# The second dense layer of a fused attention and rational FFN kernel: all blocks in float16 parts, scales from bounds on GpSimd, a new order

## The chip, the cores and the metric

The kernel runs on one core of a Trainium2 chip. The metric is the device time of one execution in microseconds. The core has a matrix engine (PE, with its weight loads PEld), a vector engine (DVE), a scalar engine (ACT), GpSimd (POOL) and a queue engine (SP). Each works through its own instructions in order, and semaphores join them. PE multiplies from SBUF into the eight banks of PSUM.

## The reference

```
# q, k, v: batch 8, heads 8, sequence 576, head size 64
scores = q @ k^T / 8
scores = where(scores >= max(scores) - tau, scores, -1e9)       # tau = 0.02
attn = exp(scores - max); attn = attn / (sum(attn) + 1e-9)
x = (attn @ v), heads side by side: 4608 tokens x 512
h = x @ w_in                                                    # 512 x 2048
P = a0 + a1 h + a2 h^2 + a3 h^3;  Q = 1 + |b0| |h| + |b1| h^2
out = (P / (Q + 1e-6)) @ w_out                                  # 2048 x 512
```

All inputs are float32. The weights come as raw 64-bit words (float32 values widened), which the kernel decodes on the chip.

## The kernel before, in words

**Attention.** Two heads of a batch make a pair; a pair has four full tiles of 128 query rows and a short one of 64, so there are 160 units of (pair, tile). For each, PE forms the scores (lines 805, 812, 816), DVE takes the row maxima (822 for two heads, 824 for a short tile), ACT applies threshold and exponential (837, 841), and the result is split into a float16 high part (`hi`, helper lines 326 and 328) and a low part (863, in place in `e`). SP's queue transposes both with DMAs into `pT`, and PE multiplies with v's parts (934). The output is stored as two float16 parts `x` (944, 950); the short tiles of four batches share one buffer `xr`. The first four pairs take another way with float32 transposes on PE (886 to 917).

**Dense layers.** The tokens are worked in 18 chunks of 256: two per batch (`m`) and two of short rows (`r`, four batches each). A chunk has four steps of four blocks (128 hidden columns each). In a step PE makes h from `x` and `wi`, both in float16 parts, with three products per block and quarter (line 1051, 48 matmuls of 256 columns a step). ACT takes h out of PSUM into one of eight buffers `t` (1060). DVE and ACT work out P/Q: |h| (1065 or 1067), r and q (1071, 1074, 1084, 1087 to 1093), log and exp for the reciprocal (1078, 1081). The second layer sums into two banks: one block of four is multiplied as plain float32 (1114), the other three as fp32r parts (1110), for which `g` is split in pieces of 256 columns: a cast (318 on ACT, 320 on DVE) and a low part (1101).

**Weights.** Each of 32 tiles is loaded on GpSimd's queue and decoded on ACT and DVE. A tile of w_in gets its size (544 or 546), a scale per group of four over a small PE product (431 to 440), and two float16 parts (326 or 328, and 562). A tile of w_out stays float32, or is cast and subtracted into two fp32r parts (592).

**Order.** All work is given to a planner as operations with a key, a duration, the engines that may do it and the buffers that it takes. The planner lays them out by its own clock, and each engine's instructions stand in that order in the program. Its parameters are constants at the head of the file: `WHEN` is the key of each weight group, `SPACING` that between dense steps, `START`, `EARLY` and `PRICE` weigh ACT against DVE for work that either can do, and `LAST` lists the chunks whose steps get keys behind the attention. Before, these were all three chunks left in the last batch (two `m` and the second `r`).

Lines that the working uses, with their numbers:

```
1051  nc.tensor.matmul(d, wi_tile(c, f0 + j, hl), x[:, c, :], ...)          # 3 parts x 4 quarters
1101  nc.vector.tensor_tensor(fr(g[:, 1]), box["r"][:, j * CT:(j + 1) * CT], g[:, 0], ALU.subtract)
1110  nc.tensor.matmul(acc[tt], fr(g[:, x]), fr(wo[f][y]), ...)             # 3 products of fp32r parts
1114  nc.tensor.matmul(acc[tt], box["r"][:, o:o + P], wo[f], ...)           # float32
```

Of the kernel before, what the change touches and what calls it, by code (L numbers as in the profile page):

```python
# [9 lines left out]
F32R = mybir.dt.float32r  # L10
# [16 lines left out]
POOLS = {"e": 3, "hi": 2, "pT": 2, "st": 8, "sc": 2, "t": 8, "u": 3, "g": 2, "x": 3, "xr": 1}  # L27
# [4 lines left out]
LEAD, SPACE0, SPACING = 4.776489494, 2.7365, 2.085146464  # L32
ENDK, ENDS = 4.7452, 10.130284218

WHEN = [(-4.7413, 1.6268), (5.5534, 0.8332), (13.0267, 0.2709), (15.0744, 0.5122)]

V0, V1 = -3.870384768, -4.680004432
# [6 lines left out]
LAST = (0, 1, 2)  # L44
# [12 lines left out]
PARTS = 3  # L57
# [5 lines left out]
PLAIN = (0, 1, 2, 3, 4)  # L63
# [4 lines left out]
AHEAD_RANK = 2.6679  # L68
# [43 lines left out]
class Hold:  # L112
# [3 lines left out]
    def __init__(self, pool, uses, sets=None):  # L116
        self.pool, self.uses, self.until, self.sets, self.bank, self.slot = pool, uses, 0.0, sets, None, None


class Plan:  # L120
# [28 lines left out]
    def spot(self, h, t):  # L149

        if h.sets is None:
            slots = self.pools[h.pool]
            return min(slots) if slots else None
        got = [(max([t] + [self.banks[i] for i in b]), n, b) for n, b in enumerate(h.sets)
               if all(self.banks[i] is not None for i in b)]
        return min(got)[::2] if got else None

    def sooner(self, e, t, o, free, can):
        price = START if t < START_END else EARLY if t < EARLY_END else PRICE
        for x, dur in o.engs.items():  # L160
            if x != e:
                begin = max(free[x], o.ready[x])
# [5 lines left out]
    def order(self):  # L168
# [21 lines left out]
        while left:  # L190
# [60 lines left out]
            for h in o.drop:  # L251
# [5 lines left out]
                elif not h.uses:  # L257
                    self.pools[h.pool].append((h.until, h.slot))
# [18 lines left out]
def masked_attention_rational_ffn(  # L277
# [54 lines left out]
    def tensor_tensor(dst, x, y, how):  # L332
# [28 lines left out]
    ones = bass.AP(one.tensor, one.offset, [list(one.ap[0]), [0, P]])  # L361

# [26 lines left out]
    def monic():  # L389
# [6 lines left out]
        nc.vector.tensor_tensor(t, b1, t, ALU.max)  # L396
        nc.vector.reciprocal(u, t)
# [14 lines left out]
    def scale_ops(key, get, up, inv, s, after, ahead=0.0):  # L412
# [20 lines left out]
        def f3():  # L433
            p2 = box["p2"]
            nc.vector.tensor_reduce(box["m2"], box["all"], AX.X, ALU.max)
            nc.vector.tensor_single_scalar(p2.bitcast(I32), box["m2"].bitcast(I32), 0x7F800000, ALU.bitwise_and)
            nc.vector.tensor_scalar(p2, p2, 2.0 ** -40, 2.0 ** 100, ALU.max, ALU.min)
# [30 lines left out]
    def decode_ops(i, key, load, hold, dst=None):  # L468
# [49 lines left out]
        o6 = op(FLEX["f6"], 0, key, f6, [o4, o2], (), [ht] if dst is None else [ht, hold])  # L518
# [778 lines left out]
```

## Time and profile before

| | us |
|---|---|
| median of 3 runs (1277.5 to 1283.15) | 1280.21 |
| the profiled execution | 1281.68 |
| its span, first to last instruction | 1279.9 |
| PE busy, 9252 matmul records | 1246.4 |
| DVE busy, 1960 instructions | 1199.3 |
| ACT busy, 2180 instructions | 1074.5 |
| POOL busy | 231.3 |

The granted clock of PE is 0.994 over the span. In a row of a stretch stand its bounds and length, then each engine's busy time with its count of instructions, the granted clock, the share of the DMA engines and GB/s. A row of a group has line, engine, operation, tiles written and read, shapes and count, then busy time and mean length in ns, then the idle time ahead of it and what ended that. A row of the timeline or of the chain of waits begins with start and length in us.

### The profile page before, as it was taken

To read this page: it belongs to the slowest core of one execution; us is meant where nothing else is said; L and a number is where in the kernel's file an instruction comes from. 1 tells how busy PE (TensorE), PEld (TensorE's weight loads), DVE (VectorE), ACT (ScalarE), POOL (GpSimd) and SP (SyncE) were. 2 spreads that over 40 slices of the span, in tenths; PEclk is the share of its full clock that TensorE was granted. 3 is DMA by queue.
4 is the path that set the end of the run, shared out by engine and by line. 5 is a ranking of instruction groups with operands and counts; after the bars stand their busy time and mean duration, and the time that the engine had idled before them with its cause. 6 is when DMAs were issued, how large, how long until landed. Compare 5 with 4: busy or idle time off the path is not lost.

```text
span 1279.9 us, 25127 instructions
## 1 busy us (share of the span) xinstructions
PE 1246.4 (97%) x9252; PEld 889.8 (70%) x9252; DVE 1199.3 (94%) x1960; ACT 1074.5 (84%) x2180; POOL 231.3 (18%) x480
## 2 busy tenths in 40 slices
PE   8899999999999999999999999999999999999998
PEld 6576676676767667766667667677776667677775
DVE  5899999999999999999999899999999999997876
ACT  5999888989999888888897699999988998874454
POOL 2112000132132311332022140322121221100000
PEclk9999999999999999999999999999999999999999
DMA  7645246688667656776442765876566665530000
GB/s 216 174 143 163 78 105 112 134 144 154 105 133 132 146 107 119 142 137 126 91 105 56 131 141 111 142 135 136 104 120 125 130 123 112 111 71 17 18 17 17
DMA packets 338251, 146.64 MB, mean 115 GB/s; under 512 B 314416, under 2 KB 320720, under 8 KB 338128
## 3 DMA queue, kind: packets, MB, share of 16 engines
q1 hardware_dynamic: 316528, 87.67, 38.5%
q0 software_dynamic: 21280, 56.78, 16.4%
q8 instruction: 73, 1.20, 0.4%
q10 hardware_dynamic: 320, 0.59, 0.2%
q14 instruction: 50, 0.41, 0.1%
HBM read 60.30 MB, written 9.44 MB: 54 GB/s over the span
## 4 chain that ended last, share of the span: by engine, by line
PE 53%; DVE 27%; ACT 8%; issue 5%; DMA 3%; SPq 0%; DVEq 0%; ACTq 0%
PE banks L1051 16%; PE banks L1110 15%; PE banks L1114 6%; PE banks L934 6%; PE banks L816 5%; DVE e L863 4%; DVE st L822 3%; DMA pT<-e 2%; DVE t L1071 2%; DVE t L1087 2%; DVE t L1090 2%; PE banks L805 2%; DVE t L1084 2%; DVE t L1093 2%; DVE g L1101 2%
## 5 line engine op out<-in xcount | busy, mean ns | idle before, releaser
L1051 PEld LDWEIGHTS <-wi 128*128 128x128 f16 x3456 | 324.1, 98 | 144.1 <-issue 108.0
L1051 PE MATMUL banks<-x,wi 128*128 128x256 f16 x3072 | 374.7, 275 | 3.0 <-ACT t L1060 1.7
L1110 PE MATMUL banks<-wp,g 128*128 128x512 f32 x1296 | 355.2, 415 | 1.9 <-ACT g L318 1.2
L1110 PEld LDWEIGHTS banks<-wp,g 128*128 128x128 f32 x1296 | 234.0, 189 | 70.9 <-issue 15.5
L837 ACT ACTIVATE e<-banks,st 128x576 f32<-128x576 f32 x288 | 206.4, 735 | 18.5 <-DVE st L831 11.1
L841 ACT ACTIVATE e<-e,cf 128x576 f32<-128x576 f32 x288 | 221.0, 774 | 0.3
L863 DVE SCALAR_TENSOR_TENSOR e<-e,st,hi 128x576 f16<-128x576 f32 x252 | 203.5, 808 | 3.9 <-ACT hi L326 3.4
L822 DVE TENSOR_REDUCE st<-banks 128x2 f32<-128x1152 f32 x128 | 171.8, 1342 | 12.9 <-PE banks L816 10.8
L326 ACT ACTIVATE hi<-e,st 128x576 f16<-128x576 f32 x177 | 134.0, 769 | 51.9 <-DVE st L852 41.1
L816 PE MATMUL banks<-KK,QQ 64*128 64x512 f32 x512 | 144.5, 641 | 0.0
L1114 PE MATMUL banks<-wp,t 128*128 128x512 f32 x288 | 142.2, 608 | 1.7 <-DVE t L1093 1.6
L1060 ACT ACTIVATE t<-banks,hsc 128x512 f32<-128x512 f32 (+1 forms) x192 | 106.3, 575 | 25.9 <-PE banks L1051 24.7
L934 PEld LDWEIGHTS <-V 128*64 128x64 f16 x2520 | 104.1, 111 | 33.8 <-issue 32.6
L934 PE MATMUL banks<-pT,V 128*64 128x256 f16 (+1 forms) x2520 | 118.9, 249 | 3.0 <-DMA pT<-e 3.0
L1087 DVE SCALAR_TENSOR_TENSOR t<-t,co,t 128x1024 f32<-128x1024 f32 (+1 forms) x73 | 92.0, 1261 | 22.7 <-ACT t L1081 22.7
L1078 ACT ACTIVATE t<-t,co 128x1024 f32<-128x1024 f32 (+1 forms) x73 | 82.7, 1133 | 12.8 <-DVE t L1084 12.7
L1093 DVE SCALAR_TENSOR_TENSOR t<-t,co,t 128x1024 f32<-128x1024 f32 (+1 forms) x73 | 92.0, 1261 | 0.5
L1071 DVE SCALAR_TENSOR_TENSOR t<-t,co 128x1024 f32<-128x1024 f32 (+1 forms) x73 | 92.0, 1260 | 0.0
L1084 DVE SCALAR_TENSOR_TENSOR t<-t,co,t 128x1024 f32<-128x1024 f32 (+1 forms) x73 | 91.9, 1260 | 0.0
L1074 DVE SCALAR_TENSOR_TENSOR t<-t,co 128x1024 f32<-128x1024 f32 (+1 forms) x73 | 91.9, 1259 | 0.0
L1101 DVE TENSOR_TENSOR g<-t,g 128x256 fp32r<-128x256 f32 x216 | 86.6, 414 | 2.0 <-ACT g L318 1.6
L1090 DVE SCALAR_TENSOR_TENSOR t<-t,t 128x1024 f32<-128x1024 f32 (+1 forms) x73 | 87.7, 1201 | 0.4
(137 smaller groups left out, 1518.2 us busy)
## 6 DMA issues: line engine op xcount, KB each, us to landing
KK<-in_kT_dram POOLq DMA_DIRECT2D x84, 144.0 KB, 3.9
t<-in_w_in_dram POOLq DMA_DIRECT2D x16, 512.0 KB, 5.8
t<-in_w_out_dram POOLq DMA_DIRECT2D x16, 512.0 KB, 4.7
V<-in_v_dram POOLq DMA_DIRECT2D x24, 256.0 KB, 4.4
out_dram<-u POOLq DMA_DIRECT2D x24, 256.0 KB, 2.7
QQ<-in_qT_dram POOLq DMA_DIRECT2D x42, 144.0 KB, 3.1
QQ<-in_qT_dram POOLq DMA_DIRECT2D x42, 128.0 KB, 3.4
KK<-in_kT_dram SPq DMA_DIRECT2D x24, 144.0 KB, 3.5
```

The lines of the kernel that those rows point to most:

```text
L326: nc.scalar.activation(dst, src, AF.Identity, scale=factor)
L816: nc.tensor.matmul(d, QQ[r, t * P:(t + 1) * P], KK[r, REM:S], **one)
L822: nc.vector.tensor_reduce(box["st"][:, 0:2], box["both"], AX.X, ALU.max, negate=True)
L837: nc.scalar.activation(ev(hh), box["s"][hh], AF.Prelu, scale=SCALE, bias=box["st"][:, 2 + hh:3 + hh], alpha=STEEP)
L841: nc.scalar.activation(e, e, AF.Exp, scale=passes, accum_out=box["st"][:, 4 + hh:5 + hh])
L863: nc.vector.scalar_tensor_tensor(box["lo"][:, c], ev(hh), box["st"][:, 6 + hh:7 + hh], box["hi"][:, c], ALU.mult, ALU.subtract)
L934: nc.tensor.matmul(dst, V[:, c * P + head * D:c * P + (head + 1) * D], rhs, start=c == 0 and n == 0, stop=c == NT and n == 2)
L1051: nc.tensor.matmul(d, wi_tile(c, f0 + j, hl), x[:, c, :], start=c == 0 and n == 0, stop=c == NC - 1 and n == 2)
L1071: nc.vector.scalar_tensor_tensor(box["r"], box["h"], a2, box["h"], ALU.add, ALU.mult)
L1087: nc.vector.scalar_tensor_tensor(box["q"], box["q"], qc, box["i"], ALU.add, ALU.mult)
L1110: nc.tensor.matmul(acc[tt], fr(g[:, x]), fr(wo[f][y]), start=begins and j == n == 0, stop=ends and j == nb - 1 and n == 2)
L1114: nc.tensor.matmul(acc[tt], box["r"][:, o:o + P], wo[f], start=begins and j == 0, stop=ends and j == nb - 1)
```

## The change

**Second layer.** Every block is multiplied as three products of float16 parts (new line 1153). g is cast into float16 (329 or 331) and its low part taken (1144) for a whole step at once, 1024 columns instead of 256, into three buffers `g` of 1024 columns. w_out is treated like w_in: size, scale per group, two float16 parts (339 or 337, and 610).

**Scales from bounds.** float16 has a small range, so g is scaled. A bound on |g| is worked out for each chunk's batch from a bound on |x|, on the columns of w_in and on the polynomial. The columns' norms come from squares that ACT leaves in bfloat16, summed by PE (596) and reduced on DVE (599 to 602). Per group of weights come seven small DVE instructions (1264 to 1270, three times in all), and per table, of which there are twelve, four on GpSimd (1293 to 1296), six on DVE (1299 to 1304) and one on ACT (1307). The scale enters through the bias of the exponential (1123), a factor at 1133 instead of -2, and the output's factor. Sizes of tiles are sums of squares on ACT in 24 cases, and maxima on DVE in eight.

**Buffers and order.** `t` has 12 slots instead of eight, in pairs that could be taken as one. In the last batch the short tiles come with the first half of the visits. `LAST` has only the second `m` chunk, whose last step is cut in two as before; the two other chunks get keys among the others. `SPACING` goes from 2.085 to 2.235, and `WHEN`, `START` and `PRICE` are set anew.

The core of the diff:

```diff
-LEAD, SPACE0, SPACING = 4.776489494, 2.7365, 2.085146464
+LEAD, SPACE0, SPACING = 4.776489494, 2.7365, 2.235134465
-LAST = (0, 1, 2)
+STEPS = {'m': (4, 4, 4, 4), 'r': (4, 4, 4, 4), 'last': (4, 4, 4, 2, 2)}
+LAST = (1,)
+REST_FIRST = (7,)
...
-             "g": ([P, 2, CT], F32), "x": ([P, 2, NP, CT], F16), "xr": ([P, 2, NP, CT], F16)}
+             "g": ([P, 2, NC * CT], F16), "x": ([P, 2, NP, CT], F16), "xr": ([P, 2, NP, CT], F16)}
...
-        def f_inv():
-            nc.scalar.activation(box["i"], box["i"], AF.Exp, scale=-1.0)
+        def f_inv(x, j0, j1):
+            i = box["i"][:, j0 * CT:j1 * CT]
+            nc.scalar.activation(i, i, AF.Exp, scale=-1.0, bias=lnr(x))
...
-        def f_gl(j):
-            g = box["g", j]
-            nc.vector.tensor_tensor(fr(g[:, 1]), box["r"][:, j * CT:(j + 1) * CT], g[:, 0], ALU.subtract)
+        def f_gl(x, j0, j1):
+            w = (j1 - j0) * CT
+            nc.vector.tensor_tensor(box["g", x][:, 1, 0:w], box["r"][:, j0 * CT:j1 * CT], box["g", x][:, 0, 0:w], ALU.subtract)
...
-            if in_parts(f):
-                g = box["g", j][:, :, tt * P:(tt + 1) * P]
-                for n, (x, y) in enumerate(((0, 0), (1, 0), (0, 1))):
-                    nc.tensor.matmul(acc[tt], fr(g[:, x]), fr(wo[f][y]), start=begins and j == n == 0,
-                                     stop=ends and j == nb - 1 and n == 2)
-                return
-            o = j * CT + tt * P
-            nc.tensor.matmul(acc[tt], box["r"][:, o:o + P], wo[f], start=begins and j == 0, stop=ends and j == nb - 1)
+            x = f // NC
+            o = (f - max(x * NC, f0)) * CT + tt * P
+            for n, (y, z) in enumerate(((0, 0), (1, 0), (0, 1))):
+                nc.tensor.matmul(acc[tt], box["g", x][:, y, o:o + P], wo[:, x, f % NC, z], start=begins and j == n == 0,
+                                 stop=ends and j == nb - 1 and n == 2)
...
+            def f_bound():
+                x = isx[:, b:b + 1] if kind == "m" else R
+                e = engines[plan.eng]
+                e.tensor_scalar(H, x, wmax, 1.0, ALU.mult, ALU.mult)
+                e.tensor_scalar(s, H, c2, H, ALU.add, ALU.mult)
+                e.tensor_scalar(s, s, c1, H, ALU.add, ALU.mult)
+                e.tensor_scalar(s, s, c0, ct, ALU.add, ALU.mult)
+
+            def f_scales():
+                nc.vector.scalar_tensor_tensor(s, H, c1s, s, ALU.add, ALU.min)
+                nc.vector.tensor_single_scalar(s.bitcast(I32), s.bitcast(I32), EVEN, ALU.bitwise_and)
+                nc.vector.tensor_scalar(s, s, SMALL, None, ALU.max)
+                nc.vector.tensor_scalar(R.bitcast(I32), s.bitcast(I32), -0.5, float(197 << 23), ALU.mult, ALU.add)
+                nc.vector.tensor_scalar(m2r, m2, R, None, ALU.mult)
+                nc.vector.tensor_scalar(down, s, dn, None, ALU.mult)
+
+            def f_ln_r():
+                nc.scalar.activation(lnr, m2r, AF.Ln, scale=-0.5)
...
+            o = op(BOUND, 0, p, f_bound, o)
+            o = op("DVE", 0.8, p, f_scales, [o])
+            o = op("ACT", 0.25, p, f_ln_r, [o])
```

What the order makes of it is shown at three places. First PE, where the attention's last product (`pT`, `V`) gives way to the dense layers alone. Before, it goes on with fp32r products (`wp_0`, `wp_1` are w_out's parts):

```order
L934 LDWEIGHTS V_165
L934 MATMUL banks<-pT_84,V_165 64x64
L1110 MATMUL banks<-wp_0_159,g_97 128x512 x2
L1110 MATMUL banks<-wp_1_160,g_97 128x512
L1110 MATMUL banks<-wp_0_159,g_97 128x512 x2
L1110 MATMUL banks<-wp_1_160,g_97 128x512
L1051 LDWEIGHTS wi
L1051 MATMUL banks<-x_100,wi 128x256
```

And now, on the same engine, with `wo` as w_out's float16 parts:

```order
L969 LDWEIGHTS V_141
L969 MATMUL banks<-pT_76,V_141 64x256
L1153 LDWEIGHTS g_88
L1153 MATMUL banks<-wo,g_88 128x512
L1153 LDWEIGHTS g_88
L1153 MATMUL banks<-wo,g_88 128x512
```

Behind this point stand 456 first-layer matmuls, 222 fp32r and 24 float32 products before, and 354 first-layer and 288 float16 products now. Behind the last scores (a little earlier) they are 552, 234 and 26 before, and 468 and 312 now.

Second, DVE in the third batch, behind the scale of v. Before, from the table of h's scales (`hsc`) it goes straight back to the attention:

```order
L863 SCALAR_TENSOR_TENSOR e_80<-e_80,st_86,hi_83 128x576
L950 SCALAR_TENSOR_TENSOR x_99<-banks,x_99 128x256
L1221 TENSOR_SCALAR hsc<-sw,isx 128x4
L852 RECIPROCAL st_87<-st_87 128x2
L822 TENSOR_REDUCE st_88<-banks 128x2
```

Now the table of the bounds (`gs`) follows it:

```order
L898 SCALAR_TENSOR_TENSOR e_72<-e_72,st_78,hi_75 128x576
L1336 TENSOR_SCALAR hsc<-sw,isx 128x4
L1299 SCALAR_TENSOR_TENSOR gs_m_0_4_156<-gs_m_0_4_156,co 128x1
L1300 TENSOR_SCALAR gs_m_0_4_156<-gs_m_0_4_156 128x1
L1301 TENSOR_SCALAR gs_m_0_4_156<-gs_m_0_4_156 128x1
L1302 TENSOR_SCALAR gs_m_0_4_156<-gs_m_0_4_156 128x1
L1303 TENSOR_SCALAR gs_m_0_4_156<-gc_4_151,gs_m_0_4_156 128x4
L1304 TENSOR_SCALAR gs_m_0_4_156<-gs_m_0_4_156,gc_4_151 128x1
```

Six instructions are new in DVE's row there; the first waits for POOL, each other one for the one ahead of it.

Third, POOL's queue at the same place, which before held loads of k, q and v alone (`KK`, `QQ`, `V`):

```order
L688 DMA KK_116<-in_kT_dram 64x576
L1293 TENSOR_SCALAR gs_m_0_4_156<-isx,gc_4_151 128x1
L1294 TENSOR_SCALAR gs_m_0_4_156<-gs_m_0_4_156,co 128x1
L1295 TENSOR_SCALAR gs_m_0_4_156<-gs_m_0_4_156,co 128x1
L1296 TENSOR_SCALAR gs_m_0_4_156<-gs_m_0_4_156,co 128x1
L724 DMA V_141<-in_v_dram 128x4x128
```

The first of the four waits for DVE's scale of v (`isx`), and the load of v stands behind them.

More of the change, by code (lines that the diff above doesn't have):

```diff
@@ L242, in order @@
                     slots = self.pools[h.pool]
-                    h.slot = min(slots)[1]
-                    slots.remove(min(slots))
+                    h.slot = self.spot(h, t)[1]
+                    slots[:] = [x for x in slots if x[1] != h.slot and not (h.wide and x[1] == h.slot + 1)]
                 else:
@@ L257, in order @@
                 elif not h.uses:
-                    self.pools[h.pool].append((h.until, h.slot))
+                    self.pools[h.pool] += [(h.until, h.slot + i) for i in range(1 + h.wide)]
             for d in o.then:
@@ L410, in masked_attention_rational_ffn, with bounds, scale_ops @@
     co = op("DVE", 2.1, 6.0, monic, [co])
-    def scale_ops(key, get, up, inv, s, after, ahead=0.0):
+    def bounds():
+        nc.vector.tensor_single_scalar(co_[:, 9:12].bitcast(I32), co_[:, 0:3].bitcast(I32), 0x7FFFFFFF, ALU.bitwise_and)
+        nc.vector.tensor_scalar(c1s, ct, 1.0, 0.25, ALU.add, ALU.mult)
+        nc.vector.scalar_tensor_tensor(c1s, c1s, c1, c2, ALU.mult, ALU.add)
+        nc.vector.scalar_tensor_tensor(c1s, c0, ct, c1s, ALU.mult, ALU.add)
+    co_b = op("DVE", 0.4, 6.0, bounds, [co])
+    def scale_ops(key, get, up, inv, s, after, ahead=0.0, squares=False, mask=MASK):
         box = {}
@@ L603, in masked_attention_rational_ffn @@
         v0 = bb * NP
-        if bb < VISITED:
+        if bb in REST_FIRST:
+            visits += [(v0 + i, half + rest) for i in range(NP - 1)] + [(v0 + NP - 1, half + rest + other)]
+            visits += [(v0 + i, other) for i in range(NP - 2, -1, -1)]
+        elif bb < VISITED:
             visits += [(v0 + i, half) for i in range(NP - 1)] + [(v0 + NP - 1, half + other + rest)]
@@ L670, in is_plain @@
     def is_plain(bp, t):
-        return bp < NP and t in PLAIN
+        return t in PLAIN.get(bp, ())
     v_ops = {}
@@ L1008, in unit_ops @@
         x_first.setdefault(ck, av)
-        xh = op(FLEX["xh" if full else "xhr"], 0, p + 1.4, f_xh, [av, isx_done["up"]] + ([x_done[ck][0]] if not first else []), (), [bh])
+        xh = op(FLEX["xh" if full else "xhr"], 0, p + 1.4, f_xh, [av, isx_done.get(("up", bb))] + ([x_done[ck][0]] if not first else []), (), [bh])
         xl = op("DVE", 0.335 if full else 0.134, p + 1.5, f_xl, [xh], (), [bh])
@@ L1028, in moe_ops, with can, slow, mid @@
         FW = nb * CT
+        parts = [(x, max(x * NC, f0) - f0, min(x * NC + NC, f0 + nb) - f0) for x in range(g, (f0 + nb - 1) // NC + 1)]
         box = {}
-        def can(kind):
-            return {e: size(e, d) for e, d in FLEX[kind].items() if e == "DVE" or not soon}
-        def size(e, d):
-            return d + (nb / 2 - 1) * (d - {"ACT": 0.18, "DVE": 0.08}[e])
-        def on(e, d, *rest):
-            return op(e, size(e, d), *rest)
+        def can(n, act, dve):
+            return {"DVE": dve(n)} if soon else {"ACT": act(n), "DVE": dve(n)}
+        def slow(n):
+            return 0.129 + n * 0.2667
+        def mid(n):
+            return 0.068 + n * 0.2667
+        def fast(n):
+            return 0.07 + n * 0.1333
+        def act(n):
+            return 0.098 + n * 0.2133
         bhs = [Hold("b", 1 if kind == "m" else 4, BH if p < end else BH + [(i,) for i in B3[0]]) for _ in range(nb // 2)]
```

362 lines of the change are left out of this document (217 added, 145 removed).

## The prediction

> **What bounds the kernel now.** I read the page's busy shares first, then busy time by stretch, with cuts where the start ends (184 us), around the largest stall (690 to 760), and at the last row maximum of the attention (1132.96 us, line 824).
>
> ```profile
> PE 1246.4 (97%) x9252; PEld 889.8 (70%) x9252; DVE 1199.3 (94%) x1960; ACT 1074.5 (84%) x2180; POOL 231.3 (18%) x480
> ```
> ```profile
> core 0: us, PE busy (x) PEld busy (x) DVE busy (x) ACT busy (x) POOL busy (x), PEclk, DMA share, GB/s
> 0.00:184.00 184.00, 168.30 (x1227) 124.32 (x1228) 160.00 (x374) 160.22 (x343) 30.10 (x77) 0.98 0.52 149
> 160.00:480.00 320.00, 317.58 (x2456) 223.80 (x2454) 317.50 (x497) 290.75 (x588) 61.16 (x125) 1.00 0.65 127
> 184.00:690.00 506.00, 501.25 (x3774) 352.24 (x3772) 496.67 (x772) 451.27 (x926) 105.04 (x210) 1.00 0.64 124
> 690.00:760.00 70.00, 64.95 (x531) 45.82 (x530) 62.08 (x104) 53.39 (x109) 19.85 (x41) 0.98 0.64 120
> 760.00:1132.96 372.96, 370.99 (x2830) 261.06 (x2829) 363.38 (x570) 336.55 (x677) 76.36 (x152) 1.00 0.63 120
> 1132.96:1279.90 146.94, 140.90 (x898) 106.41 (x896) 117.15 (x147) 73.06 (x129) 0.00 (x0) 0.99 0.10 25
> ```
>
> Two engines bound it together. Up to 1132.96 us DVE works 1082.1 us (160.00 + 496.67 + 62.08 + 363.38) and idles 50.8: 24.0 in the start, 26.8 after it. PE is as full from 184 us on. Behind 1132.96 us only the dense layers are left, and there PE works 140.9 of 146.9 us while DVE idles 29.8: that tail belongs to PE. So the change is costed as DVE's work up to the last maximum, DVE's idle time ahead of it, and the tail.
>
> **PE.** The chain of work that ended last shows rows back to back:
>
> ```profile
> 901.88 3.94 PE banks L1051 x36
> 1160.30 1.72 PE banks L1114 x4
> 1162.02 2.80 PE banks L1110 x12
> ```
>
> A first-layer matmul (float16, 256 columns) takes 3.94/36 = 0.1094 us, a second-layer product in fp32r parts (512 columns) 2.80/12 = 0.2333, a float32 product 0.86 (two records each, so x4 is two products). A step of four blocks had 18 fp32r and two float32 products, 4.20 + 1.72 = 5.92 us; now it has 24 of float16 with 512 columns. No row shows those. The nearest is L1051, per column: 0.2188 each, 5.25 a step, 0.67 less; as an upper bound they cost 0.2333. I take 0.2188. Over 72 steps PE sheds 48 us. New are 16 column sums and four small products (about 5 us, in the start, beside DVE's decoding) and 50 warming matmuls in gaps. PE so has slack ahead of the last maximum, and its gain there shows only as waits that DVE no longer has.
>
> **DVE** gets more work. Its rows overlap: the start of one 1024-wide instruction follows the last by 1.19 us where the record says 1.28, so I price each at its mean less 0.08.
>
> ```profile
> 1144.79 1.28 DVE L1071 SCALAR_TENSOR_TENSOR t<-t,co 128x1024 f32<-128x1024 f32 x1
> 1145.98 1.28 DVE L1074 SCALAR_TENSOR_TENSOR t<-t,co 128x1024 f32<-128x1024 f32 x1
> ```
> ```profile
> L1101 DVE TENSOR_TENSOR g<-t,g 128x256 fp32r<-128x256 f32 x216 | 86.6, 414 | 2.0 <-ACT g L318 1.6
> L320 DVE CAST g<-t 128x256 fp32r<-128x256 f32 x93 | 25.7, 285 | 2.2 <-PE banks L1110 1.5
> L592 DVE TENSOR_TENSOR wp<-t,wp 128x512 fp32r<-128x512 f32 x12 | 8.2, 683 | 0.1
> L320 DVE CAST wp<-t 128x512 fp32r<-128x512 f32 x8 | 3.5, 436 | 0.0
> L1090 DVE SCALAR_TENSOR_TENSOR t<-t,t 128x1024 f32<-128x1024 f32 x71 | 86.3, 1215 | 0.4
> L1067 DVE TENSOR_SCALAR t<-t 128x1024 int32<-128x1024 int32 x12 | 8.3, 688 | 1.5 <-ACT t L1060 1.4
> L562 DVE SCALAR_TENSOR_TENSOR wi<-t,sw,wi 128x512 f16<-128x512 f32 x16 | 11.6, 745 | 0.0
> L328 DVE TENSOR_SCALAR wi<-t,sw 128x512 f16<-128x512 f32 x10 | 4.5, 478 | 0.0
> L437 DVE TENSOR_SCALAR sc<-sc 128x1 f32<-128x1 f32 x12 | 1.8, 153 | 0.4
> ```
>
> Counts are of rows in the order. Gone: 216 low parts of g (x 0.334 = 72.1), 93 casts of g (19.1), 12 low and 8 high parts of w_out (7.2 + 2.8): 101.2 us. New: 73 low parts of whole steps, 71 at L1090's 1.135 and two at 0.60 (81.8); 24 wide casts, priced by L1067 (14.3); 16 low parts of w_out at 0.665 (10.6); three more high parts of weights in sum (1.2); four more scale chains (1.1 each, 4.4) and four column norms (4.3); 99 tiny instructions for scale tables, each waiting for the one before, as L437 does, at 0.153 (15.2); seven more decoding pieces and size maxima (5.6). That is 137.4. Absolute values drop from 13 to 5 (8 x 0.608 = 4.9), and what the order gives to ACT instead (three maxima of v, six high parts of the attention, some copies) saves 8.5. Sum: 137.4 - 101.2 - 13.4 = +23 us. Bounds: the 16-bit results may go at half L1067's price (-7) or the wide casts at L1090's (+12). Behind the last maximum DVE has 107.5 us of rows instead of 113.8, so the 6 less there means **+29 ahead of it: 1111 us**.
>
> **ACT** gains 38 us (13 squares at L544's price, 8 absolute values, 13 high parts of weights, 6 of the attention): 1112 us, 87% of the span, not a bound; its casts of g, 123 narrow or 48 wide, cost the same.
>
> ```profile
> L318 ACT CAST g<-t 128x256 fp32r<-128x256 f32 x123 | 47.8, 401 | 41.9 <-PE banks L1110 35.7 <-DVE t L1093 5.3
> L1065 ACT ACTIVATE t<-t 128x1024 f32<-128x1024 f32 x59 | 62.3, 1055 | 0.3
> L544 ACT ACTIVATE t<-t 128x512 f32<-128x512 f32 x11 | 7.6, 692 | 3.1 <-DVE t L333 3.1
> ```
>
> **GpSimd** gets 48 tiny instructions, four for each of 12 tables, between DVE's scale of v and the join at line 1299 on DVE. Behind them on its queue stand loads of v, Q and K for later units. The trace has a lone tiny one at 0.18 us and one that took 1.98 while DVE ran without a gap:
>
> ```profile
> 115.98 1.98 POOL L483 TENSOR_SCALAR cf<-t 1x1 f32<-1x1 f32 x1 [0.27 <-DMA t<-in_w_out_dram]
> 118.52 0.18 POOL L483 TENSOR_SCALAR cf<-t 1x1 f32<-1x1 f32 x1
> 116.56 0.75 DVE L1101 TENSOR_TENSOR g<-t,g 128x256 fp32r<-128x256 f32 x2
> ```
>
> The join has 6 to 8 us of DVE rows ahead of it in most batches. If GpSimd is held off that long, DVE comes to the join, waits, and so frees it: 4 x 0.18 = 0.7 us. Between 0 and 12 x 0.7 = 8.6 us I take 1.8, most joins being covered; POOL's own loads wait no longer than that, which the idle POOL hides.
> The Trainium skill (SBUF — State Buffer, "Who interferes with whom") says that GpSimd and DVE share one pair of ports, locked for a whole instruction, and whoever comes second is blocked. The 1.98 us agrees for GpSimd as the second; that DVE is ever the one to wait, no row here shows.
>
> **DVE's idle time ahead of the last maximum.** The start: 24 us before; ACT and DVE both get about 15 us more to do in it, which lengthens the work and leaves the gaps; I keep 24 (20 to 30). After it: 26.8 before. With PE relieved, DVE is the only full engine, as it nearly was from 160 to 480 us, where it idled 2.5 of 320 us, 0.8%. At that rate 949 us give 7.4; with the 1.8 of the joins 9 us. Bounds 3 and 27.
>
> **The tail.** It starts with the last scores (PE, 1131.63 us).
>
> ```profile
> 1131.63 1.29 PE L805 MATMUL banks<-KK,QQ 128*128 128x512 f32 x4
> 1132.96 0.76 DVE L824 TENSOR_REDUCE st<-banks 128x1 f32<-128x576 f32 x1
> 1224.22 1.29 DVE L1087 SCALAR_TENSOR_TENSOR t<-t,co,t 128x1024 f32<-128x1024 f32 x1 [1.97 <-ACT t L1081]
> ```
>
> PE had behind them 552 first-layer matmuls (60.4), 234 fp32r (54.6), 26 float32 (22.4) and 2.2 of the attention: 139.6. Now 468 (51.2), 312 of float16 (68.3) and 3.5: 123.0, 16.6 less. DVE's 107.5 and waits of 2 us for ACT, as in L1087's row, stay below that where two steps are interleaved. So 146.9 - 16.6 = 130.
>
> **Sum.** 1111 + 24 + 9 + 130 = 1274 us of span; outside it lie 1.8 us (1281.68 - 1279.9), and the median of the runs is 1.5 below the profiled execution: **1274.3 us**, 0.5% below 1280.21. Half a per cent is about what a measurement tells from no change.
>
> **Rivals.**
> *The stalls stay (slower).* DVE's idle time of 690 to 760 us came from a late transposing DMA, not from PE:
>
> ```profile
> 702.12 10.68 DMA pT<-e
> 708.89 0.77 ACT L326 ACTIVATE hi<-e,st 128x576 f16<-128x576 f32 x1 [6.30 <-DMA pT<-hi]
> 709.70 0.82 DVE L863 SCALAR_TENSOR_TENSOR e<-e,st,hi 128x576 f16<-128x576 f32 x1 [2.60 <-ACT hi L326]
> ```
>
> The transposes and buffers are unchanged. If DVE idles 27 us again, it is 1292; it turns slower above 21 us. Against it: a single full engine has more work queued to cover a late one.
> *GpSimd holds DVE up.* If each of the 48 gets in first, DVE loses 48 x 0.18 = 8.7 us: 1283. For: line 1299 waits each time; against: the DVE rows beside the 1.98 have their usual length. The Trainium skill's page named above would allow it.
> *PE was the cause of more.* From 760 us PE idled 2.0 of 373 us while DVE idled 9.6. If DVE's idle falls to 3 and the tail loses 5 more, since scores no longer queue behind products: 1263.
> *The float16 products run at fp32r's pace.* The tail gets 312 x 0.0145 = 4.5 longer: 1279.
>
> **How the numbers follow.** The forecast (idle 3 to 14, 1268 to 1279) has 0.45, the stalls 0.20, GpSimd 0.10, PE as the cause 0.20, no gain in pace 0.05. Faster by over 0.5% (below 1273.8): 0.25 of the forecast and PE's 0.20, 0.45. Slower (above 1286.6): 0.18 of the stalls, 0.02 of GpSimd, 0.20. The rest, 0.35, is no change. The range, 1260 to 1292, ends at the stalls and a little below PE's case; the forecast's own is 1268 to 1279.
>
> **What would show it.** PE busy near 1200 and 24 float16 products in 5.25 us; DVE busy near 1222, with about 33 us idle ahead of the last maximum and 130 us from there to the end. It is wrong if DVE idles over 45 us ahead of it, if line 1299 waits for POOL, if the tail's steps follow DVE's chain and not PE, or if DVE's work is not 20 us more.

## The result and the profile after

The changed kernel takes 1288.7 us (median of seven runs, 1284.67 to 1291.92) against 1279.35 for the kernel before on the same chip (seven runs, 1276.14 to 1283.15): ratio 1.0072, 95% interval 1.0052 to 1.0093. It is slower by 0.7%, where 1274.3, 0.5% faster, was forecast. The profiled execution is the median one, 1288.7 us with a span of 1286.9.

First the busy shares of the page, then busy time by stretch, cut as before and at the new place of the last row maximum (line 857, at 1160.86 us):

```profile
PE 1225.7 (95%) x9520; PEld 799.3 (62%) x9520; DVE 1224.1 (95%) x1871; ACT 1114.2 (87%) x2183; POOL 262.4 (20%) x528
```
```profile
0.00:184.00 184.00, 164.26 (x1119) 115.37 (x1120) 154.34 (x397) 157.81 (x349) 29.59 (x79) 0.94 0.45 135
184.00:690.00 506.00, 490.01 (x3948) 319.85 (x3946) 500.63 (x726) 458.55 (x896) 117.92 (x229) 0.99 0.63 123
690.00:760.00 70.00, 61.84 (x508) 37.34 (x507) 63.87 (x86) 61.09 (x131) 19.78 (x41) 0.95 0.63 125
760.00:1160.86 400.86, 387.44 (x3113) 247.66 (x3111) 395.11 (x561) 365.55 (x704) 95.13 (x181) 0.98 0.61 118
1160.86:1286.90 126.04, 122.19 (x840) 79.11 (x838) 110.11 (x106) 71.16 (x107) 0.00 (x0) 1.00 0.12 29
```

The third busy column is DVE's. Up to the last maximum it works 154.34 + 500.63 + 63.87 + 395.11 = 1113.95 us and idles 29.7 in the start (184 - 154.34) and 17.2 after it. The tail is 126.0, with PE at work in 122.2 of it. So the prediction's own sum reads:

| term | before | predicted | after | off by |
|---|---|---|---|---|
| DVE's work ahead of the last maximum | 1082.1 | 1111 | 1113.9 | +2.9 |
| DVE's idle time in the start | 24.0 | 24 | 29.7 | +5.7 |
| DVE's idle time from 184 us to the last maximum | 26.8 | 9 | 17.2 | +8.2 |
| tail | 146.9 | 130 | 126.0 | -4.0 |
| span | 1279.9 | 1274 | 1286.9 | +12.9 |

DVE got 31.8 us more to do on the path. The tail paid 20.9 of them back, and idle time only 3.9. The miss is in the two rows of idle time.

**The start.** What DVE waited for up to 184 us (total, times, longest), before and then after:

```profile
DVE vm L704 <- DMA V<-in_v_dram: 4.2, 1, 4.2
```
```profile
DVE vm L737 <- DMA V<-in_v_dram: 8.9, 4, 4.0
...
DVE gs_m L1299 <- POOL gs_m L1296: 1.0, 1, 1.0
```

And the queue that brings the weights (q0: packets, MB, share) with the loads of v (count, KB, median us to landing), both up to 40 us, before and then after:

```profile
q0 software_dynamic: 1364, 5.00, 38.8%
...
V<-in_v_dram SPq DMA_DIRECT2D x5, 256.0 KB, 5.3
```
```profile
q0 software_dynamic: 1728, 6.29, 49.6%
...
V<-in_v_dram SPq DMA_DIRECT2D x5, 256.0 KB, 8.2
```

With 12 slots of `t` GpSimd sends 12 loads of weights in the first 35 us with no wait above 3.6 us; with eight it stood still for 9.2 us after the fifth. 1.3 MB more come by 40 us, and v is 2.9 us later. The longer waits for v (4.7 us) and one join of a scale table (1.0) are together the 5.7 us by which the start is off.

**After the start.** Gaps of under 1 us in DVE's row, added up from the rows, are 8.8 us before and 9.0 now. Longer ones fell from nine with 18.0 us to four with 8.3. These four are two joins of the scale tables and two waits behind a late transposing DMA:

```profile
DVE gs_r L1299 <- POOL gs_r L1296: 2.3, 2, 1.3
```
```profile
1041.50 1.79 POOL L1293 TENSOR_SCALAR gs_r<-gs_r,gc 128x1 f32<-128x1 f32 x1
1043.39 1.26 POOL L1294 TENSOR_SCALAR gs_r<-gs_r,co 128x1 f32<-128x1 f32 x1
1044.75 0.34 POOL L1295 TENSOR_SCALAR gs_r<-gs_r,co 128x1 f32<-128x1 f32 x1
```
```profile
714.06 8.65 DMA pT<-hi
```
```profile
723.60 0.82 DVE L898 SCALAR_TENSOR_TENSOR e<-e,st,hi 128x576 f16<-128x576 f32 x1 [3.97 <-ACT hi L337]
732.32 1.36 DVE L857 TENSOR_REDUCE st<-banks 128x2 f32<-128x1152 f32 x1 [1.99 <-PE banks L851]
```

GpSimd's instructions, priced at 0.18 us, take 0.25 (L1293) or 0.34 us (L1294 to L1296) at their shortest here and up to 2.48 while DVE is busy. Of the two waits behind the transpose the first is direct: ACT's high part in line 337 waits for it, and DVE for ACT. The second is put down to it, since PE had idled for 6.8 us meanwhile. The late transpose has a twin before, the 10.68 us at 702.12 on which the rival *the stalls stay* rested; waits of 2.6 and 2.3 us followed that one.

The traces show what the two have in common. Beside both, GpSimd sends the loads of v for two pairs within a few us of each other (here at 714.28 and 717.38 us), and these are late as well: first v's loads on GpSimd's queue from 690 to 740 us, then over the whole span (count, KB, median us to landing).

```profile
V<-in_v_dram POOLq DMA_DIRECT2D x2, 256.0 KB, 7.5
```
```profile
V<-in_v_dram POOLq DMA_DIRECT2D x24, 256.0 KB, 4.4
```

In the traces of all 16 kernels here, 30 of the 38 transposes that were under way beside more than three of v's transfers (a pair's load is three) took over 7 us, 51 of 863 beside one to three, and 12 of 3579 beside none. No run moved these loads, so this shows what goes together and not the cause.

### The profile page after: what moved, and what is told of

Its sections match the earlier page's. It is cut to its first block, busy times and chain, and to the rows that moved or that the text cites. A ratio compares the mean times of both kernels' runs of the same rounds, so it can differ in the third digit from the quotient of the medians.

```text
span 1286.9 us, 25594 instructions
## 1 busy us (share of the span) xinstructions
PE 1225.7 (95%) x9520; PEld 799.3 (62%) x9520; DVE 1224.1 (95%) x1871; ACT 1114.2 (87%) x2183; POOL 262.4 (20%) x528
## 4 chain that ended last, share of the span: by engine, by line
PE 29%; DVE 22%; issue 6%; ACT 5%; POOL 1%; DMA 1%; DVEq 0%; ACTq 0%; POOLq 0%
PE banks L1153 12%; PE banks L1092 11%; DVE e L898 5%; PE banks L969 3%; DVE st L857 3%; PE banks L851 3%; DVE g L1144 2%; DVE t L1126 1%; DVE t L1129 1%; DVE t L1112 1%; DVE t L1115 1%; DVE t L1133 1%; DVE t L1136 1%; ACT e L872 1%; DVE hi L339 1%
## 5 line engine op out<-in xcount | busy, mean ns | idle before, releaser
L1153 PE MATMUL banks<-wo,g 128*128 128x512 f16 x1728 | 401.7, 381 | 8.0 <-DVE g L1144 8.0
L1092 PEld LDWEIGHTS <-wi 128*128 128x128 f16 x3456 | 335.2, 99 | 109.6 <-issue 57.8
L1092 PE MATMUL banks<-x,wi 128*128 128x256 f16 x3072 | 362.3, 275 | 19.3 <-ACT t L1101 16.7
L1153 PEld LDWEIGHTS <-g 128*128 128x128 f16 x1728 | 162.5, 99 | 226.7 <-issue 40.9
L872 ACT ACTIVATE e<-banks,st 128x576 f32<-128x576 f32 x288 | 208.6, 736 | 12.6 <-DVE st L866 9.9
L337 ACT ACTIVATE hi<-e,st 128x576 f16<-128x576 f32 x183 | 139.0, 768 | 49.5 <-DVE st L887 38.4
L851 PE MATMUL banks<-KK,QQ 64*128 64x512 f32 x512 | 148.5, 658 | 0.0
L1101 ACT ACTIVATE t<-banks,hsc 128x512 f32<-128x512 f32 (+1 forms) x192 | 106.4, 573 | 18.1 <-PE banks L1092 17.7
L680 POOL DMA_DIRECT2D QQ<-in_qT_dram x42 | 22.2, 529 | 341.5 <-PE banks L840 192.6
L1144 DVE TENSOR_TENSOR g<-t,g 128x1024 f16<-128x1024 f32 (+1 forms) x73 | 87.6, 1200 | 0.1
L1126 DVE SCALAR_TENSOR_TENSOR t<-t,co,t 128x1024 f32<-128x1024 f32 (+1 forms) x65 | 81.7, 1257 | 0.0
L1129 DVE SCALAR_TENSOR_TENSOR t<-t,co,t 128x1024 f32<-128x1024 f32 (+1 forms) x62 | 77.9, 1257 | 1.9 <-ACT t L1123 1.9
L1136 DVE SCALAR_TENSOR_TENSOR t<-t,co,t 128x1024 f32<-128x1024 f32 (+1 forms) x63 | 79.2, 1257 | 0.1
L724 POOL DMA_DIRECT2D V<-in_v_dram x24 | 18.8, 785 | 272.0 <-PE banks L969 169.8
```

Of the source, the lines that this page charges most:

```text
L337: nc.scalar.activation(dst, src, AF.Identity, scale=factor)
L851: nc.tensor.matmul(d, QQ[r, t * P:(t + 1) * P], KK[r, REM:S], **one)
L872: nc.scalar.activation(ev(hh), box["s"][hh], AF.Prelu, scale=SCALE, bias=box["st"][:, 2 + hh:3 + hh], alpha=STEEP)
L1092: nc.tensor.matmul(d, wi_tile(c, f0 + j, hl), x[:, c, :], start=c == 0 and n == 0, stop=c == NC - 1 and n == 2)
L1101: nc.scalar.activation(box["h3"][:, 2 * k:2 * k + 2, sl], psv[:, :, sl], AF.Identity, scale=hsc[:, b2, (f0 + 2 * k) // NC:(f0 + 2 * k) // ...
L1144: nc.vector.tensor_tensor(box["g", x][:, 1, 0:w], box["r"][:, j0 * CT:j1 * CT], box["g", x][:, 0, 0:w], ALU.subtract)
```

## The experiments

All kernels were timed in five rounds against the kernel before on their chip. The columns are the median, the ratio to before with its interval, and, from one profiled execution, DVE's work and idle time up to the last maximum, and the tail. Idle time is a stretch's length less DVE's busy time. The profiled execution of e6 is its longest, 1318.0 us; the others lie within 3 us of their medians.

| kernel | us | ratio | DVE work | idle, start | idle, later | tail |
|---|---|---|---|---|---|---|
| after | 1288.7 | 1.0072 (1.0052 to 1.0093) | 1113.9 | 29.7 | 17.2 | 126.0 |
| e1, tables left out | 1272.5 | 0.9937 (0.9912 to 0.9961) | 1106.1 | 26.9 | 13.7 | 125.4 |
| e2, two products | 1281.0 | 1.0006 (0.9990 to 1.0023) | 1112.9 | 28.3 | 17.7 | 120.9 |
| e3, 8 slots of t | 1304.3 | 1.0178 (1.0152 to 1.0203) | 1123.8 | 28.4 | 26.3 | 123.4 |
| e4, old order | 1303.8 | 1.0178 (1.0154 to 1.0202) | 1128.1 | 32.3 | 16.1 | 123.8 |
| e5, tables on GpSimd | 1304.9 | 1.0196 (1.0177 to 1.0215) | 1104.3 | 30.8 | 43.2 | 125.4 |
| e6, more on ACT | 1310.7 | 1.0226 (1.0205 to 1.0247) | 1107.1 | 33.0 | 51.3 | 124.8 |
| e7, e5 and e6 | 1329.1 | 1.0375 (1.0358 to 1.0391) | 1096.9 | 39.2 | 65.8 | 124.8 |
| e8, LAST as before | 1292.2 | 1.0090 (1.0076 to 1.0103) | 1115.0 | 29.3 | 13.4 | 132.7 |
| e9, bound on DVE | 1298.9 | 1.0143 (1.0123 to 1.0163) | 1125.2 | 27.0 | 16.8 | 125.4 |
| e10, two loads in flight | 1284.2 | 1.0034 (1.0023 to 1.0045) | 1114.3 | 23.4 | 18.9 | 125.4 |
| e11, linear bound | 1280.7 | 1.0002 (0.9992 to 1.0011) | 1112.6 | 25.2 | 14.4 | 125.4 |
| e12, e10 and e11 | 1276.6 | 0.9986 (0.9969 to 1.0003) | 1112.4 | 23.1 | 14.5 | 125.5 |
| e13, before, two in flight | 1279.6 | 0.9997 (0.9982 to 1.0012) | 1081.5 | 22.1 | 27.6 | 147.0 |
| e14, e12 with one in flight | 1293.2 | 1.0103 (1.0079 to 1.0127) | 1113.4 | 37.2 | 14.8 | 125.5 |

In e1, e2, e5, e9, e10, e11, e12 and e14 every other instruction stands in the changed kernel's order, and in e13 in that of the kernel before; in the others the planner laid everything out anew.

**e1.** GpSimd's part returns at once, and of DVE's six instructions two are left.

```diff
-                e.tensor_scalar(H, x, wmax, 1.0, ALU.mult, ALU.mult)
-                ... (three more on GpSimd, four on VectorE)
-                nc.vector.tensor_scalar(m2r, m2, R, None, ALU.mult)
+                nc.vector.tensor_scalar(m2r, m2, one, None, ALU.mult)
...
```

> The changed kernel without the work of the 12 scale tables: GpSimd's four tiny instructions of each table and four of VectorE's six are left out, the factors are constants; the order on every engine is otherwise the same. Profile of the changed kernel: VectorE works 1113.9 us ahead of the last row maximum, idles 46.9, and the tail is 126.0, span 1286.9. Theory A (VectorE's work ahead of the last maximum is the bound, and the sum is short by its idle time): 48 tiny instructions of 0.16 us leave it, 7.8 us, and with them the 3.3 us in which line 1299 waited for GpSimd; span about 1276, VectorE's other idle time as it was. Rival B (GpSimd holds VectorE up beyond these waits): VectorE's other rows get shorter too, span 1270 or less. Rival C (the time is set by transfers and by the order, VectorE's work is absorbed): idle time takes up what is saved, span 1283 to 1287.

Busy time by stretch (start, then to the last maximum at 1146.70, then the tail):

```profile
0.00:184.00 184.00, 165.44 (x1148) 115.32 (x1148) 157.07 (x401) 160.25 (x353) 27.87 (x79) 0.96 0.47 139
184.00:1146.70 962.70, 930.82 (x7538) 600.76 (x7537) 948.98 (x1319) 881.05 (x1724) 200.61 (x401) 0.99 0.64 122
```

The span fell by 14.8 us to 1272.1: 7.9 of work, 6.3 of idle time and 0.6 in the tail. Work taken off DVE in an unchanged order is paid in full, and more; C is out. DVE's other rows are as long as they were, so B's reason does not hold either, though the span is near B's. The idle part is larger than the 3.3 us of joins: 2.8 of it lies in the start, where four kernels with the changed kernel's order of the first 100 us (e1, e2, e9, e11) read 25.2 to 28.3, so that some 2 us of it are the spread of single executions.

**e2.** The product with w_out's low part is left out.

```diff
-            for n, (y, z) in enumerate(((0, 0), (1, 0), (0, 1))):
+            for n, (y, z) in enumerate(((0, 0), (1, 0))):
...
```

> The changed kernel with two products instead of three in the second layer (the one with w_out's low part is left out); the order on the other engines is the same. 576 products at 0.2158 us, 124 us, leave TensorE, 104 of them (22.4 us) behind the last scores. Theory A: TensorE is not what VectorE waits for any more; the last row maximum stays within 5 us of 1160.9, and only the tail changes, until VectorE's 108 us of work and its 7 idle set it: about 116 instead of 126, span about 1277. Rival D (VectorE's idle time still comes from TensorE's queue): the waits of line 857 for line 851 (9.9 us) and a part of the small gaps go as well, the last maximum comes 10 to 15 us earlier, span 1262 to 1267.

Busy time from the start's end to the last maximum, and of the tail:

```profile
184.00:1158.80 974.80, 867.66 (x7100) 558.35 (x7099) 957.14 (x1367) 883.21 (x1726) 232.66 (x447) 0.98 0.63 121
1158.80:1279.70 120.90, 105.19 (x732) 68.80 (x730) 109.81 (x107) 70.28 (x107) 0.00 (x0) 0.95 0.12 31
```

PE works 867.7 of 974.8 us, and DVE idles 17.7 as with PE full: the last maximum comes 2.1 us earlier, not 10 to 15. Rival D is out. Ahead of the last maximum PE's slack has no use left; in the tail 22.4 us off PE gave 5.1, since DVE's 109.8 and the waits between the two engines then set it.

**e3.** Fewer slots.

```diff
-POOLS = {..., "t": 12, ...}
+POOLS = {..., "t": 8, ...}
```

> The changed kernel with 8 slots of t instead of 12; the planner lays all out anew (rows priced by the changed kernel's profile: VectorE +7.7 us ahead of the last maximum, 4.8 less behind; TensorE 4.5 less behind the last scores). Theory A for the start: 12 slots let 12 loads of weights go out in the first 35 us where 8 held them at 24.5, and these delay the loads of v (8.2 us to landing against 5.3 before), for which VectorE waits 8.9 us against 4.2. With 8 slots the loads of v land in 5 to 6 us and VectorE's idle time up to 184 us falls from 29.7 to about 24; span 1113.9 + 7.7 + 41.2 + 121.5 = 1284. Rival E (the waits for v come from the maxima being placed early, not from traffic): idle time of the start stays near 30, span about 1290. Rival F (the steps need the slots): VectorE idles over 25 us after 184 us instead of 17, span above 1292.

Weights and v's landing up to 40 us, then DVE's waits over the whole span:

```profile
q0 software_dynamic: 1152, 4.19, 33.5%
...
V<-in_v_dram SPq DMA_DIRECT2D x5, 256.0 KB, 5.5
```
```profile
DVE t L1129 <- ACT t L1123: 12.8, 7, 2.5
...
DVE vm L737 <- DMA V<-in_v_dram: 5.2, 3, 3.6
DVE st L883 <- ACT e L876: 5.0, 5, 1.3
```

v lands early again and DVE's waits for it fall from 8.9 to 5.2, as A said. The start as a whole gained only 1.3, and F came true: steps with fewer slots are less interleaved, and DVE waits for ACT's exponential (12.8 us). The slots are needed; only what they let out early is not.

**e4.** All numbers of the order as before (`LAST`, `REST_FIRST`, `SPACING`, `WHEN`, `V0`, `V1`, `START`, `START_END`, `EARLY_END`, `PRICE`, `AHEAD_RANK`).

```diff
-LEAD, SPACE0, SPACING = 4.776489494, 2.7365, 2.235134465
+LEAD, SPACE0, SPACING = 4.776489494, 2.7365, 2.085146464
...
-LAST = (1,)
+LAST = (0, 1, 2)
...
```

> The changed kernel's arithmetic with the order's numbers of before: LAST with all three chunks, short rows last, the old SPACING, WHEN, V0, V1, START, EARLY_END and PRICE. Rows priced by the changed kernel's profile: VectorE works 13.0 us more ahead of the last maximum (1126.9) and 14.2 less behind; TensorE has 106.8 us of matmuls behind the last scores instead of 118.5. Theory A (work and not order is what costs): idle 47 as now, tail 114, span 1288, within 4 us of the changed kernel. Rival G (the new order is what costs the time, the arithmetic gains): idle time falls to some 35, span 1277 or less.

Busy time up to the last maximum, and of the tail:

```profile
0.00:1176.40 1176.40, 1117.79 (x8768) 729.09 (x8769) 1128.06 (x1771) 1049.35 (x2089) 267.00 (x532) 0.98 0.59 122
1176.40:1300.20 123.80, 111.03 (x756) 70.07 (x754) 95.67 (x96) 64.58 (x100) 0.00 (x0) 0.99 0.08 21
```

The arithmetic in the old order costs 20.3 us of span; the new order takes 13.3 of that back. It does so by the place of DVE's work: 110.1 us of it lie behind the last maximum instead of 95.7, beside a tail that PE sets. G is out, and A's size was wrong: its 114 us of tail took PE's rows, and PE does work 111.0 us there, but it also waits, mostly for g (6.8 us for its casts on ACT and low parts on DVE), and the tail is 123.8.

**e5.** The whole table on GpSimd.

```diff
-                nc.vector.tensor_scalar(m2r, m2, R, None, ALU.mult)
+                nc.gpsimd.tensor_scalar(m2r, m2, R, 1.0, ALU.mult, ALU.mult)
...
```

> The changed kernel with the whole chain of each of the 12 scale tables on GpSimd (ten tiny instructions there, the power of 4 found by integer steps; none of VectorE's six is left), the order on the other engines the same. Leaving four of the six and GpSimd's part out took 14.8 us of span: 7.8 of VectorE's work and 7 of its idle time. Theory A (the join and VectorE's tiny instructions are the cost): VectorE loses 72 tiny ones, 11.5 us (1102.4 ahead of the last maximum), idles 40 or 41, tail 126, span about 1269. Rival B (GpSimd's instructions hold VectorE up through what the two share): 120 of them at 0.18 us, up to 21 us, come back as longer rows or idle time, span 1280 or more.

One of the ten instructions (shortest, median and longest in ns), and waits of ACT and DVE over the span:

```profile
L1294 POOL TENSOR_SCALAR gs_m<-gs_m,co x10: 336/636/3587, 111.0 to 1049.4; 128x1 f32<-128x1 f32 x10
```
```profile
ACT gs_m L1307 <- POOL gs_m L1303: 19.9, 9, 4.5
...
DVE st L887 <- ACT st L881: 16.0, 7, 5.6
...
ACT gs_r L1307 <- POOL gs_r L1303: 9.3, 2, 5.4
```

DVE works 9.6 us less and the time is 16 us longer. DVE is not held: its rows are as long as in the changed kernel, to under 1 us in all. GpSimd is: an instruction of 0.34 us takes up to 3.59. ACT's one instruction of the table stands in its row and waits 29.2 us for the table, and behind it on ACT stand the attention's row sums (line 881) and high parts, for which DVE waits. The Trainium skill (SBUF — State Buffer, "Who interferes with whom") has whoever comes second on the ports that the two share blocked; that agrees for GpSimd, and no run here shows it for DVE.

**e6 and e7.** Other weights for work that either engine can do, alone and with e5.

```diff
-EARLY = {"ACT": 2.0183, "DVE": 2.9268}
+EARLY = {"ACT": 1.8, "DVE": 3.6}
```

> The changed kernel with other weights for work that ScalarE or VectorE can do (EARLY 1.8 and 3.6 instead of 2.0183 and 2.9268), which gives ScalarE more of it: by the changed kernel's rows VectorE has 17.9 us less ahead of the last maximum and 8.2 less behind, ScalarE 39.7 more (1154). Theory A (VectorE's work is the bound): it works 1096 ahead of the last maximum, idles 47, tail 474 x 0.1094 + 288 x 0.2158 + 7.5 = 121.5, span 1265. Rival C (waits set the time): VectorE's idle time takes back at least half, as ScalarE's queue is longer, span 1276 to 1287.

> The two edits of e5 and e6 together: VectorE 1096 - 11.5 = 1084.5 us of work ahead of the last maximum. Theory A: they add, idle 41, tail 121.5, span 1247. Rival C: ScalarE, at 1154 us, and TensorE begin to hold VectorE up; idle 55, span 1261 or more.

DVE's waits over the span of e6:

```profile
DVE st L857 <- PE banks L851: 18.6, 23, 5.4
DVE t L1129 <- ACT t L1123: 18.2, 11, 2.5
DVE st L883 <- ACT e L876: 12.5, 13, 2.9
```

Rival C, and by more than it said: DVE works 6.8 us less and idles 37.4 more, of which up to 7 can be the spread of this long execution. In the changed kernel these three waits are 9.9, 4.3 and 1.1 us. ACT, busy for 1147 us, answers later, and the loop from DVE over ACT and PE back to DVE (maximum, exponential, next scores) waits at every turn; how much of it the new layout brought is not shown. e7's loss, 40 us of median, is about the sum of the two (16 and 22).

**e8.** Only `LAST` and the short rows as before.

```diff
-LAST = (1,)
-REST_FIRST = (7,)
+LAST = (0, 1, 2)
+REST_FIRST = ()
```

> The changed kernel with LAST of all three chunks and short rows last again; the other numbers of the order as changed. With all of the old order the span was 1300.2, VectorE working 14.3 us more ahead of the last maximum. By the changed kernel's rows VectorE has 2.5 us more ahead of the last maximum here (1116.4) and 3.9 less behind; TensorE 408 x 0.1094 + 312 x 0.2158 = 112.0 us behind the last scores. Theory A: idle 47, tail 119.5, span 1283. Rival H (LAST and the short rows are what the new order's 13 us come from, through idle time in the last batch): idle 55 or more, span 1294 to 1300.

The span is 1290.4, between A and H, and neither's reason holds in full: idle time ahead of the last maximum is 4.2 us less and the tail 6.7 longer, with PE at work in 119.3 of 132.7 us. So these two edits alone make up 3.5 of the 13.3 us of e4.

**e9.** The bound on DVE, at the same places.

```diff
-                e = engines[plan.eng]
+                e = nc.vector
```

> The changed kernel with the four tiny instructions of each scale table's bound on VectorE instead of GpSimd, at the same places of an otherwise unchanged order. Without them and four of VectorE's six the span was 14.8 us shorter: 7.8 of VectorE's work, 7.0 of its idle time. Theory A (the idle part comes from GpSimd being late: 5.8 us from the first to the join where the planner allows 1.8, and then ScalarE's line 1307 and what stands behind it): VectorE works 48 x 0.16 = 7.7 us more ahead of the last maximum (1121.6) and idles 7 less (40), span 1287 to 1288, as now. Rival I (the idle part comes from dependent tiny instructions themselves, each waiting for the one ahead): it grows instead, span 1295 or more.

One of the four in its new place (busy, mean ns | idle ahead):

```profile
L1294 DVE TENSOR_SCALAR gs_m<-gs_m,co 128x1 f32<-128x1 f32 x10 | 2.7, 273 | 0.4
```

With two 128x1 operands for scalars it takes 0.273 us instead of 0.16, so DVE has 11.3 us more, not 7.7. Idle time fell by 3.1 and not by 7, and by place most of that is not the joins: 2.7 lie in the start, where executions of this order differ by about as much, and 0.4 behind it, where the joins had 2.3. So GpSimd's lateness costs 3 us at most; leaving the bound to DVE costs more than that.

**e10.** GpSimd lets two loads of weights be in flight.

```diff
-AHEAD = 3
+AHEAD = 2
```

> The changed kernel with two loads of weights in flight in the start instead of three (AHEAD 2; GpSimd waits for the last but one to land before the next goes out); the order on all other engines is the same. Theory A (loads of weights crowd those of v): v's loads land in 5 to 6 us instead of 8.2, VectorE waits 4 us for them instead of 8.9, idle time of the start 25 instead of 29.7, span 1282. Rival J (the weights are needed as early as they come): VectorE or ScalarE wait for decoding instead, start's idle time 30 or more, span 1287 or more.

```profile
q0 software_dynamic: 1433, 5.22, 43.2%
...
V<-in_v_dram SPq DMA_DIRECT2D x5, 256.0 KB, 5.8
```
```profile
DVE vm L737 <- POOL cf L518: 2.1, 1, 2.1
```

These are the weights and v's landing up to 40 us, and what is left of DVE's waits at line 737 beside 0.4 us for v itself. As A said, or better: waits at line 737 of 2.5 us where A had 4, start's idle time 23.4, span 1282.0. The two intervals of the ratio, 1.0023 to 1.0045 here and 1.0052 to 1.0093 for the changed kernel, do not meet.

**e11.** The looser of the two bounds alone, so that GpSimd is not asked.

```diff
-                nc.vector.scalar_tensor_tensor(s, H, c1s, s, ALU.add, ALU.min)
+                nc.vector.tensor_scalar(s, x, wmax, c1s, ALU.mult, ALU.add)
...
```

> The changed kernel with the looser of the two bounds on |g| alone (linear in the bound on |x|): GpSimd's four instructions of each table go, and VectorE has five instead of six, the first of which needs only the scale of v; the order is otherwise the same. Leaving out GpSimd's part and four of the six took 14.8 us. Theory A: of that, three of the four tiny instructions come back (36 x 0.155 = 5.6 us), span 1272.1 + 5.6 = 1278; VectorE works 1111.7 ahead of the last maximum and idles 40 or 41. Rival I (dependent tiny instructions cost twice their record): 11 us come back, span 1283 to 1285.

1277.6 us of span where A had 1278. 8 us of median thus go with five tiny instructions of each of 12 tables (four of GpSimd, one of DVE), though DVE's work falls by only 1.3 us: the rest is idle time, 4.5 in the start (of which some is spread, as said at e1) and 2.8 after it.

**e12.** Both edits.

> The edits of e10 and e11 together, the rest of the order as in the changed kernel: the linear bound alone, so that GpSimd has no part in the scale tables and VectorE five tiny instructions for each, and two loads of weights in flight instead of three. Theory A (both costs are separate: the tables' join and GpSimd's lateness, and the crowding of v's loads): VectorE works 1112.7 us ahead of the last maximum, idles 23.5 in the start and 14 after it, tail 125.5, span 1276, median 1278 or a little less, below both kernels. Rival K (what e11 gained in the start, 25.2 instead of 29.7, was the same time as e10's): no more than 1 us below e11. If they add in full, 1277.6 - 4.9 = 1273.

1276.6 us, 1% below the changed kernel, with a span of 1275.5 where A had 1276. The ratio to before fell by 0.0038 with e10 and by 0.0070 with e11, and falls by 0.0086 with both. Against the kernel before it is 0.9986, with an interval that holds 1: no measurable gain. Nor is rival K ruled out: by the ratios e12 is 2.0 us below e11, and their intervals overlap.

**e13 and e14.** The pacing of e10 in the kernel before, and one step further in e12 (AHEAD 1).

> The kernel before with two loads of weights in flight in the start instead of three (AHEAD 2), all else as it was. In it 5.0 MB of weights have come by 40 us and v lands in 5.3 us; in the changed kernel 6.3 MB and 8.2 us, and 5.2 MB and 5.8 us with AHEAD 2. Theory A (the 12 slots brought the crowding; with 8 slots POOL is held by the slots anyway): no more than 2 us gained, idle time of the start 22 to 24, ratio 0.998 to 1.002. Rival L (the traffic was a cost before as well): VectorE's wait of 4.2 us for v goes, start's idle 20 or less, ratio 0.997 or less.

> The kernel of e12 with one load of weights in flight instead of two. Theory A (at two, v is no longer held up, 5.5 us to landing and 2.8 us of waits, so that less traffic brings nothing and later weights cost): start's idle time above 23.1, ScalarE and VectorE wait for decoding, span 1276 to 1282. Rival M (traffic still sets the start): v lands in 5 us or less, start's idle 20, span 1272.

DVE's waits for v in the start of e13, and in e14 what took their place:

```profile
DVE vm L704 <- DMA V<-in_v_dram: 4.0, 1, 4.0
```
```profile
DVE u L538 <- ACT u L528: 11.0, 5, 4.7
...
DVE u L530 <- DMA t<-in_w_out_dram: 2.6, 1, 2.6
```

The kernel before does not gain. The edit takes no traffic away there (5.3 MB by 40 us, v in 5.2 us), as A had it: its eight slots already hold the loads back, and the crowding came with the change. With one load in flight v lands in 3.5 us, and decoding waits for weights instead; the start idles 37.2. Both went A's way, the second with a price that A had put too low.

## Why the prediction was wrong

- **DVE's work: right.** +24.8 us in all where +23 was worked out, 1113.9 ahead of the last maximum for 1111. e1 shows that such work, taken off in an unchanged order, counts at least one for one.
- **ACT: right.** +39.7 for +38, and no bound. That it has no room to take work from DVE (e6) was not in question there, but 87% busy reads as if it had.
- **PE: right in price, and its gain had no use.** A step's 24 products take 5.18 us for the 5.25 taken (chain of waits):

```profile
1194.57 5.18 PE banks L1153 x24
```

  PE busy is 1225.7, not near 1200. The 50 warming matmuls, named there without a price, are 11 to 14 us of that, and the column sums and small products some 3 more than the 5 taken; the granted clock of the span is 0.981 where it was 0.994, and what it adds was not taken apart. e2 shows that less work on PE changes little ahead of the last maximum.
- **The tail: right, 4 us better.** 126.0 for 130, and PE sets it as forecast.
- **The start, "I keep 24": the step that failed first.** It counted the work that the start gets and kept the gaps. The diff had 12 slots of `t` in it; what they would send out early, and past what, was not asked. Idle time grew by 5.7 us in the profiled execution, and by 3.4 in the mean of five executions (27.4: after, e1, e2, e9 and e11, of which e1, e9 and e11 lack the join); 23.4 and 23.1 us are left when the loads are held back (e10, e12), and the same edit does nothing measurable to the kernel before (e13).
- **After the start, "0.8%, as from 160 to 480 us": the step that failed second.** That stretch had no wait for a late DMA and no table. The rate itself was nearly right: gaps under 1 us are 9.0 us where it gave 7.4. But the late transpose, which the rival had named, was put at nothing on the argument that a full engine has work queued to cover it; DVE ran out of work behind it, and the waits near 724 and 732 us are 6.0. The joins took 2.3, and 1.0 more in the start, where 1.8 was taken for all, with GpSimd's instructions at 0.18 us instead of 0.34 and more. *The stalls stay* was right about the late transpose and half right in size: 17.2 us of 26.8. That the time came out near its 1292 is in part chance: the start, which that rival left at 24, brought 5.7 us of the miss.
- ***GpSimd holds DVE up*: wrong in its mechanism.** GpSimd is held up, and what waits for it is late: 3.3 us at the joins, and far more where ACT waits too (e5).
- ***PE was the cause of more*: wrong** (e2). ***The float16 products run at fp32r's pace*: wrong**, by the row above.

The single runs' median lies at the profiled execution and not 1.5 us below it, which is the rest of the difference between 1274.3 and 1288.7. Of the prediction's own signs of being wrong two came: DVE idles 46.9 us ahead of the last maximum, and line 1299 waits for POOL. What stays open is which part of e1's and e11's gain in the start is spread between executions, and whether v's loads of two pairs are what makes the transpose late; neither was tried.

## What to carry to other kernels

When a change gives a pool more slots, look at the queue that fills it: what goes out earlier is a cost to whatever lands at the same time, until the loads are paced by hand. In a kernel whose engines are all 85% busy and more, price idle time by the waits of the whole stretch, late transfers included, not by its quietest part; relief for the second engine does not remove them. And a helper engine's small instructions are to be priced with the whole range that the trace shows, and the in-order engines behind them counted as waiters.

## What the runs showed of the hardware

- A GpSimd instruction on 128x1 (line 1294 of e5) takes 0.34 us when alone, the same in the middle of a row maximum on DVE (482.5 and 1049.4 us), and 3.59 beside a run of DVE's 1024-wide instructions (111.0 us); 120 of GpSimd's instructions lengthened DVE's rows by under 1 us in all.
- A DVE instruction on 128x1 takes 0.154 us with constants, 0.207 with one 128x1 operand for a scalar (line 1304 of the changed kernel) and 0.273 with two (e9).
- In each of the 16 kernels one transposing DMA sent between 698 and 750 us takes 7.5 to 12.6 us, 8.7 in the changed kernel, beside v's loads of two pairs; the median transpose with no load of v under way takes 3.2.
